# Linear attention and two dense layers: grouped small products, a third fill bank, a reciprocal kept in PSUM, later output transposes

## The chip, the cores and the metric

One NeuronCore of a Trainium2 chip runs the whole kernel. The metric is the device time of one execution in microseconds (us). Five engines work side by side, each with its own queue of instructions: TensorE (PE, with its weight loads shown apart as PEld), VectorE (DVE), ScalarE (ACT), GpSimd (POOL) and SyncE (SP), which here only issues DMAs.

## The reference

Three layers follow one another (B = 4 sequences, H = 8 heads, S = 768 tokens, D = 48; 3072 tokens of 384 numbers).

```python
# 1 gated linear attention
f = 1 / (1 + exp(-f_logit))
for t in range(S):
    state = f[:, :, t, :, None] * state + einsum('bhd,bhe->bhde', k[:, :, t], v[:, :, t])
    y[:, :, t] = einsum('bhd,bhde->bhe', q[:, :, t], state)
# 2 first mix, w_in 384 x 2048, w_out 2048 x 384
h = x @ w_in
P = a[0] + a[1] * h + a[2] * h**2 + a[3] * h**3
Q = 1 + abs(b[0]) * abs(h) + abs(b[1]) * h**2
x = (P / (Q + 1e-06)) @ w_out
# 3 second mix, four experts, w1 384 x 1024, w2 1024 x 384
p = domain_probs / (domain_probs.sum(-1, keepdims=True) + 1e-09)
out = sum(p[:, e:e+1] * (maximum(x @ w1[e], 0) @ w2[e]) for e in range(4))
```

## The kernel before

The tokens go in six chunks, c = 0 to 5; a chunk is 128 time steps of each of the four sequences, so 512 columns. The main loop (L1051 on) counts steps v. Each step from 0 on makes one of the 192 tiles of the second mix (6 chunks x 4 experts x 8 tiles of 128 hidden units): **in2** is the product into the tile, **out2** the product out of it. A number in float32 is split in a high and a low part, so each product is three matmuls; in2 and out2 of a tile are nine matmuls each, 128 x 128 by 128 x 512. `mm_in` issues in2 and in1 at L849, `mm_out` issues out2 and out1 at L859.

Chunk c of the first mix is made while chunk c-1 of the second mix runs: 16 tiles (c, j), each with **in1** into the bank `h1`, a gate on ACT, DVE and POOL, and out1 for four tiles together. The attention of chunk c is woven in as well, in blocks (c, b), one for each sequence, each over six steps (`stage`): scores in the fourth; `k_t` (four transposes of k, L486) and `y_all` (56 small matmuls, L494) in the fifth; `update` (four products of two small matmuls, L528) in the sixth. `fill_run` and `fill_step` put one entry of a list behind each of the nine matmuls of a product: in the fifth stage the list is k_t in the first places (spread over the first three matmuls of out2) and `y_all` behind the sixth; in the sixth stage the four updates stand behind the third, fifth, seventh and ninth matmul of in2.

Chunk 0 has no second mix to run beside. In this **fill** phase `fill_in` (L898, three matmuls of 128 x 512) and `fill_out` (L905) do chunk 0 of the first mix, with the same gate, in float32 without a split.

PSUM has eight banks: `acc` = 0 to 2 for out1 and out2, `hb` = 3 and 4 for in2 (and for fill_in, by turns), `h1` = 5 for in1 (the order listings below call it bank_97; bank_92 is bank 0), 6 and 7 for the attention and for the transposes of the output. In the fill the gate keeps q in banks 5, 6, 7 by turns.

The **gate** of a tile (`gate_in`, `gate_step`) takes two steps. On ACT: a copy h of the bank (L914), q = square (L918), r = scaled abs (L919), y (L920). On DVE: q = Q (L934). On ACT: r = exp(-ln q) (L935, L936). One step later on DVE two refinements of the reciprocal, both reading q and r: L929, and L931 or L938. Then L943 and the split into gh (L945, ACT) and gl (L960, DVE). In the steps with no new gate the order on DVE is L929, L938, L943; the relu's split of in2 (L968 on ACT for gh, L969 on DVE for gl) is queued on the same two engines.

The **output** of chunk c is written in the first steps of chunk c+1. `write_out` (L1026) does three transposes of 128 x 128 (L1028) into bank 6 or 7, a copy to SBUF on ACT (L1035, pool `osp`, two buffers) and a DMA from SP (L1037); it is called for two sequences at a time. Chunk 0 does sequences 0, 1 in step k = 2 ahead of out2 and 2, 3 in the same step behind in2's place; chunks 1 to 4 do 0, 1 in step k = 1, and 2, 3 in step k = 2 ahead of out2. What is transposed is `o`, which POOL sums up (L1004).

Of the kernel before, what the change touches and what calls it, by code (L numbers as in the profile page):

```python
# [8 lines left out]
F32 = mybir.dt.float32  # L9
# [11 lines left out]
NCH = S // C  # L21
NP = NH // 2
# [319 lines left out]
PA, PB, ACT0, ACT1, POOL1, DVE1, REST = range(7)  # L342


def first_mix_steps():


    when, groups = {}, {}
    for c in range(1, NCH):
        p = NE * NJ2 * (c - 1)  # L350
        if c == 1:
            at = [10, 11, 12, 13, 14, 15, 16, 17, 18, 19, 20, 21, 23, 24, 25, 26]
            ends = (16, 20, 24, 29)
        else:
            at = [2, 3, 4, 5] if c == 2 else [-1, 1, 3, 5]
            at += [7, 9, 11, 13, 15, 17, 19, 21, 23, 24, 25, 26]
            ends = (8, 16, 24, 29)
        for j, s in enumerate(at):
            when[p + s] = (c, j)
        for n, s in enumerate(ends):  # L360
            groups[p + s] = (c, n)
    return when, groups
# [37 lines left out]
class Block:  # L400
# [117 lines left out]
    def y_all(self):  # L518
        if self.c:
            self.inter()  # L520
        self.intra()

    def y_parts(self):
        return [self.y_all]

# [32 lines left out]
class Att:  # L558
# [104 lines left out]
    def stage(self, blk, k):  # L663
        rs = range(NP)
        if k == 1:
            return {ACT0: [blk.exp], DVE1: [blk.w], REST: [blk.scans]}
        if k == 2:
            return {ACT0: [blk.inverse], POOL1: [blk.k_hat], DVE1: [blk.newton1], REST: [blk.newton2]}
        if k == 3:
            return {POOL1: [blk.q_hat]}  # L670
        if k == 4:
            return {PA: [blk.all_scores] + [lambda: None] * (8 * (blk.c == 1)), REST: [blk.masked]}
        wait = [lambda: None] * 3
        if k == 5:
            keys = [] if blk.last else [partial(blk.k_t, r) for r in rs]
            copy = [] if blk.last else [blk.k_copy]
            return {PB: keys + wait + blk.y_parts() + wait, REST: copy + [blk.x_hi]}
        if k == 6:
            upd = [] if blk.last else [partial(blk.update, r) for r in rs]
            return {PA: upd, DVE1: [blk.x_lo], REST: [] if blk.last else [blk.finish]}  # L680
        return {}

# [12 lines left out]
def fused(ctx, tc, aps, consts, gm, big, dp, prep, flag_op):  # L695
# [7 lines left out]
    banks = [pp.tile([128, 512], F32, name=f"bank{i}") for i in range(8)]  # L703
    acc, hb, h1 = banks[0:3], banks[3:5], banks[5]
    tok = acc + [h1]

    def pool(name, bufs):
        return ctx.enter_context(tc.tile_pool(name=name, bufs=bufs))
# [3 lines left out]
    g1p, g2p, gp = pool("g1p", QC1), pool("g2p", 3), pool("gp", 2)  # L712
# [8 lines left out]
    raw, temp, w1f = {}, {}, {}  # L721
# [37 lines left out]
    def run_late():  # L759
        for f in late:  # L760
            f()
        late.clear()

    def conv_ops(tau):
        fs = [[], []]
        for i in range(NJ1):
            for k in range(2):
                if tau == CONV1[i] + k * (CONV1[i] >= NB - 6):
                    fs[k].append(partial(conv, i, k))
        return fs  # L770
# [39 lines left out]
    def store_all():  # L810
        for k in stores:
            nc.sync.dma_start(out=scr[uses[k]], in_=tile_of[k].bitcast(F32))
        stores.clear()
# [79 lines left out]
        make_ready(state["used"] + R)  # L893

    def fill_in(j):
        w, ps = w1f[j], hb[j % 2]
        for kk in range(3):
            nc.tensor.matmul(ps, w[:, kk * 128:(kk + 1) * 128], att.x[0][:, kk, :], start=(kk == 0), stop=(kk == 2))  # L898
        gate_queue.append((0, j, ps))
# [6 lines left out]


    gate_queue, gate = [], {}

    def gate_in(u):  # L910
        h = u[2]
        if u[0]:
            h = gp.tile([128, 512], F32, tag="h", name="h")
            nc.scalar.copy(out=h, in_=u[2])  # L914
        q = gp.tile([128, 512], F32, tag="q", name="q", bufs=3) if u[0] else banks[5 + u[1] % 3]
        r = gp.tile([128, 512], F32, tag="r", name="r")
        y = gp.tile([128, 512], F32, tag="y", name="y")
        nc.scalar.activation(out=q, in_=h, func=AF.Square)  # L918
        nc.scalar.activation(out=r, in_=h, func=AF.Abs, scale=sc[:, 4:5])  # L919
        nc.scalar.activation(out=y, in_=h, func=AF.Identity, scale=sc[:, 0:1], bias=sc[:, 1:2])  # L920
        return q, r, y, h
# [104 lines left out]
    def write_out(c, b, bank):  # L1026
        for m in range(3):
            nc.tensor.transpose(bank[:, m * C:(m + 1) * C], o[c][:, m, b * C:(b + 1) * C], ident)  # L1028
        if c == NCH - 1:
            if not last:  # L1030
                last.append(sp.tile([128, NB, DM], F32, tag="s1", name="os"))
            nc.scalar.copy(out=last[0][:, b], in_=bank[:, 0:DM])
            return
        t = osp.tile([128, DM], F32, tag="os", name="os")
        nc.scalar.copy(out=t, in_=bank[:, 0:DM])  # L1035
        r0 = b * S + c * C
        nc.sync.dma_start(out=out[r0:r0 + C, :], in_=t)  # L1037
# [12 lines left out]
    for v in range(-FILL - 6, LAST + 1):  # L1050
        tau = v + FILL  # L1051
        ops = att.begin(v)
        if tau == -4:
            prep()
        if tau + 6 <= NB:
            att.first(tau + 6, conv_ops(tau) if tau + 6 < NB else [[], []], fetch)
        run_late()
        store_all()
        items = steps.get(v, [])
        lead = 1 if items and items[0][0] == "in2" and items[0][1] == v + 1 else 0  # L1060
        fill_run(ops[PA], 9 * lead)
        for item in items[:lead]:
            emit(item)
        if 0 <= v < LAST and v not in act2:
            relu(v)
        for f in ops[ACT0]:
            f()
        for u in gate_queue:
            if u[0] and u[:2] not in gate:
                gate[u[:2]] = gate_in(u)  # L1070
        if 0 <= tau + 1 < NJ1:
            fill_in(tau + 1)
        ready = [u for u in gate_queue if u[:2] in gate]
        new = ready[0] if ready else None
        if new:
            gate_queue.remove(new)
        old, pend_old = pend_old, new
        if new or old:
            gate_step(new, old, ops)
        else:  # L1080
            for f in ops[DVE1] + ops[ACT1] + ops[POOL1]:
                f()
        c, k = v // (NE * NJ2) - 1, v % (NE * NJ2)
        if v in (LAST - 4, LAST - 3):
            for b in range(2):
                write_out(NCH - 1, b + 2 * (v - LAST + 4), banks[6 + b])
        if 0 <= c < NCH - 1 and k == 2:
            for b in range(2):
                write_out(c, b + (2 if c else 0), banks[6 + b])
        fill_run(ops[PB], 9 * any(item[0] == "out2" for item in items), True)  # L1090
        for item in items[lead:]:
            if item[0] == "out2":
                emit(item)
                if run_bounds(v - 1)[1]:
                    evac2(v - 1)
        for item in items[lead:]:
            if item[0] == "in2":
                emit(item)
                if v + 1 < LAST:
                    relu(v + 1)  # L1100
        if 0 <= c < NCH - 1 and k == (1 if c else 2):
            for b in range(2):
                write_out(c, b + (0 if c else 2), banks[6 + b])
        for item in items[lead:]:
            if item[0] == "out1":
                emit(item)
        for item in items[lead:]:
            if item[0] == "in1":
                emit(item)
        for u in gate_queue:  # L1110
            if not u[0] and u[:2] not in gate:
                gate[u[:2]] = gate_in(u)
        if tau == -1:
            spread_probs()
        if 0 <= tau - 2 < NJ1:
            fill_out(tau - 2)
        for f in ops[REST]:
            f()
        if v in groups:
            evac1(*groups[v])  # L1120
        if tau + 6 >= NB:
            for f in sum(conv_ops(tau), []):
                f()
            run_late()
        if 10 <= tau and v < -1:
            make_ready(min(R - 6, 2 * (tau - 9)))
            split_to(min(AHEAD, state["ready"] - 2))
        if tau == NJ1 + 1:
            for m in range(3):
                split_x2(0, m, acc[m], nc.vector)  # L1130
            load_pb(0)
        if v >= -1:
            split_to(state["used"] + AHEAD)
        att.loads(v)
        if v == 170:
            flag_op(banks[6], banks[7])
# [178 lines left out]
```

## Time and profile before

| | |
|---|---|
| median of 3 runs | 1376.14 us (1375.05 to 1377.79) |
| the profiled execution | 1374.64 us |
| its span, first to last instruction | 1372.8 us |
| granted TensorE clock, mean | 0.991 |
| PE busy | 1331.0 us, 97% |
| DVE busy | 870.0 us, 63% |
| ACT busy | 663.0 us, 48% |
| POOL busy | 287.2 us, 21% |
| HBM | 211 GB/s over the span |

The span is what the trace shows; around it lie 1.8 us of the execution's own time. A wait is read from the idle time of an engine ahead of an instruction, with the instruction that ended it. An engine that is busy less than the span can still set the time in the places where it is late.

### The profile page before, as it was taken

The numbers are of one execution on the slowest core, as the hardware profiler recorded it, in microseconds if no ns is written. First come the engines' busy times: TensorE is split into PE (matmuls) and PEld (weight loads), VectorE is DVE, ScalarE is ACT, GpSimd is POOL, SyncE is SP. The second block draws the span as 40 slices with busy tenths as digits, with TensorE's granted clock in tenths as the row PEclk, the third lists the DMA queues.
The fourth block names the chain that finished last, engine by engine and source line by source line (L and its number), as shares of the span: only waits on it lengthen the run. The fifth ranks groups of instructions, "written<-read, shape, count | busy, mean of one in ns | idle before, by whom it ended". The sixth has DMA issues, their size and how long they took to land.

```text
span 1372.8 us, 19580 instructions
## 1 busy us (share of the span) xinstructions
PE 1331.0 (97%) x7158; PEld 1061.8 (77%) x7158; DVE 870.0 (63%) x1367; ACT 663.0 (48%) x1152; POOL 287.2 (21%) x257
## 2 busy tenths in 40 slices
PE   6799999899999999999999999999999999999998
PEld 6444788777787888788888878888888888888887
DVE  8899658677748565757666667576576555552221
ACT  4787448666536445426444435554445453431111
POOL 0233655565420020120110111001111001111010
PEclk9999999999999999999999999999999999999999
DMA  8547877677875666667655758566657666667660
GB/s 312 186 157 269 281 248 255 223 246 249 311 254 178 198 217 188 191 187 244 215 175 194 225 163 266 192 203 195 216 167 252 187 198 193 195 194 239 194 192 31
DMA packets 115704, 291.03 MB, mean 212 GB/s; under 512 B 13104, under 2 KB 28816, under 8 KB 114832
## 3 DMA queue, kind: packets, MB, share of 16 engines
q1 hardware_dynamic: 115024, 289.51, 65.2%
q8 instruction: 59, 0.97, 0.3%
q14 instruction: 45, 0.37, 0.1%
q10 hardware_dynamic: 576, 0.18, 0.1%
HBM read 240.83 MB, written 48.81 MB: 211 GB/s over the span
## 4 chain that ended last, share of the span: by engine, by line


## 5 line engine op out<-in xcount | busy, mean ns | idle before, releaser
L849 PE MATMUL bank<-x,w 128*128 128x512 f32 x2448 | 602.6, 393 | 5.1 <-DVE gl L969 5.1
L849 PEld LDWEIGHTS bank<-x,w 128*128 128x128 f32 x2448 | 455.5, 188 | 99.1 <-DVE gl L969 6.3
L859 PE MATMUL bank<-gh,w 128*128 128x512 f32 x1584 | 502.5, 397 | 5.5 <-DVE t L1003 5.5
L859 PEld LDWEIGHTS bank<-gh,w 128*128 128x128 f32 x1584 | 293.9, 189 | 70.9 <-DVE t L1003 6.8
L859 PE MATMUL bank<-gl,w 128*128 128x512 f32 x792 | 311.4, 393 | 0.0
L969 DVE SCALAR_TENSOR_TENSOR gl<-bank,gh 128x512 fp32r<-128x512 f32 x192 | 131.5, 686 | 152.9 <-ACT gh L968 152.5
L1004 POOL TENSOR_TENSOR o<-o,t 128x512 f32<-128x512 f32 x69 | 89.0, 1320 | 531.9 <-DVE t L1003 531.9
L859 PEld LDWEIGHTS bank<-gl,w 128*128 128x128 f32 x792 | 149.5, 189 | 32.0
L968 ACT ACTIVATE gh<-bank 128x512 fp32r<-128x512 f32 x192 | 113.7, 594 | 124.6 <-PE bank L849 124.6
L934 DVE SCALAR_TENSOR_TENSOR q<-q,sc,r 128x512 f32<-128x512 f32 x80 | 62.1, 776 | 144.6 <-ACT r L919 144.6
L945 ACT CAST gh<-q 128x512 fp32r<-128x512 f32 x80 | 49.2, 615 | 185.2 <-DVE q L943 185.1
L806 POOL TENSOR_TENSOR w<-rawbuf,w 128x384 fp32r<-128x384 f32 x96 | 104.5, 1115 | 89.2 <-ACT w L805 64.7
L914 ACT COPY h<-bank 128x512 f32<-128x512 f32 x80 | 46.9, 586 | 116.3 <-PE bank L849 115.8
L1021 DVE TENSOR_TENSOR s<-s,bank 128x512 f32<-128x512 f32 x45 | 30.9, 687 | 84.7 <-PE bank L859 84.6
L960 DVE TENSOR_TENSOR gl<-q,gh 128x512 fp32r<-128x512 f32 x80 | 55.9, 699 | 33.8 <-ACT gh L945 33.6
L935 ACT ACTIVATE r<-q,sc 128x512 f32<-128x512 f32 x80 | 58.0, 724 | 25.7 <-DVE q L934 19.0
L929 DVE SCALAR_TENSOR_TENSOR q<-q,r 128x512 f32<-128x512 f32 x80 | 69.5, 869 | 0.1
L920 ACT ACTIVATE y<-h,sc 128x512 f32<-128x512 f32 x80 | 64.1, 801 | 0.0
L943 DVE SCALAR_TENSOR_TENSOR q<-y,sc,q 128x512 f32<-128x512 f32 x80 | 62.2, 778 | 1.8
L936 ACT ACTIVATE r<-r 128x512 f32<-128x512 f32 x96 | 60.7, 633 | 3.1
L955 DVE SCALAR_TENSOR_TENSOR y<-y,sc,h 128x512 f32<-128x512 f32 x80 | 60.2, 752 | 2.8
L953 DVE TENSOR_TENSOR y<-y,h 128x512 f32<-128x512 f32 x80 | 57.2, 715 | 0.0
(113 smaller groups left out, 1242.6 us busy)
## 6 DMA issues: line engine op xcount, KB each, us to landing
w<-ws SPq DMA_DIRECT2D x448, 384.0 KB, 3.6
ws<-w SPq DMA_DIRECT2D x96, 384.0 KB, 4.1
raw<-in_w_dram SPq DMA_DIRECT2D x16, 768.0 KB, 6.8
rawbuf<-in_w_dram SPq DMA_DIRECT2D x64, 192.0 KB, 3.6
v<-in_v_dram SPq DMA_DIRECT2D x24, 320.0 KB, 4.5
f<-in_qkf_dram SPq DMA_DIRECT2D x24, 256.0 KB, 3.9
k<-in_qkf_dram SPq DMA_DIRECT2D x24, 256.0 KB, 4.5
q<-in_qkf_dram SPq DMA_DIRECT2D x24, 256.0 KB, 4.6
```

The lines of the kernel that those rows point to most:

```text
L806: nc.gpsimd.tensor_tensor(out=t[:, 1], in0=r, in1=t[:, 0].bitcast(F32), op=ALU.subtract)
L849: nc.tensor.matmul(ps, a[:, o], b[:, kk, :], start=(n == 0), stop=(n == 8))
L859: nc.tensor.matmul(acc[m], a[:, o], b, start=(start and n == 0), stop=(stop and n == last))
L920: nc.scalar.activation(out=y, in_=h, func=AF.Identity, scale=sc[:, 0:1], bias=sc[:, 1:2])
L929: vec.scalar_tensor_tensor(out=q0, in0=q0, scalar=QC, in1=r0, op0=ALU.add, op1=ALU.mult)
L934: vec.scalar_tensor_tensor(out=q, in0=q, scalar=sc[:, 5:6], in1=r, op0=ALU.mult, op1=ALU.add)
L936: nc.scalar.activation(out=r, in_=r, func=AF.Exp, scale=-1.0)
L943: vec.scalar_tensor_tensor(out=q0, in0=y0, scalar=sc[:, 3:4], in1=q0, op0=ALU.subtract, op1=ALU.mult)
L955: vec.scalar_tensor_tensor(out=y, in0=y, scalar=sc[:, 2:3], in1=h, op0=ALU.subtract, op1=ALU.mult)
L968: nc.scalar.activation(out=gh, in_=h, func=AF.Relu)
L969: nc.vector.scalar_tensor_tensor(out=gl, in0=h, scalar=0.0, in1=gh.bitcast(F32), op0=ALU.max, op1=ALU.subtract)
L1004: nc.gpsimd.tensor_tensor(out=o[c][:, m], in0=o[c][:, m], in1=t, op=ALU.add)
```

## The change

Four things change.

1. In the fifth stage k_t (all four) and `y_all` become one entry behind the sixth matmul of out2 (`keys_and_y`); in the sixth stage the four updates become one entry behind the fifth matmul of in2 (`all_updates`).
2. In the fill, `fill_in` goes round three banks (3, 4, 7) and q keeps two (5, 6).
3. A tile whose successor's in1 comes two steps or more later is called sparse (50 of the 80 tiles of chunks 1 to 5). Its r lies in `h1` in place of a tile in SBUF. The successor's in1 overwrites `h1`.
4. `write_out` of chunks 1 to 4 takes chunk 0's pattern: sequences 0, 1 one step later, ahead of out2, and 2, 3 in the same step behind in2's place.

```diff
--- before.py
+++ after.py
@@ -519,6 +519,15 @@
         if self.c:
             self.inter()
         self.intra()
+
+    def keys_and_y(self):
+        for r in range(0 if self.last else NP):
+            self.k_t(r)
+        self.y_all()
+
+    def all_updates(self):
+        for r in range(NP):
+            self.update(r)
 
     def y_parts(self):
         return [self.y_all]
@@ -670,13 +679,12 @@
             return {POOL1: [blk.q_hat]}
         if k == 4:
             return {PA: [blk.all_scores] + [lambda: None] * (8 * (blk.c == 1)), REST: [blk.masked]}
-        wait = [lambda: None] * 3
+        idle = [lambda: None]
         if k == 5:
-            keys = [] if blk.last else [partial(blk.k_t, r) for r in rs]
             copy = [] if blk.last else [blk.k_copy]
-            return {PB: keys + wait + blk.y_parts() + wait, REST: copy + [blk.x_hi]}
+            return {PB: 5 * idle + [blk.keys_and_y] + 3 * idle, REST: copy + [blk.x_hi]}
         if k == 6:
-            upd = [] if blk.last else [partial(blk.update, r) for r in rs]
+            upd = [] if blk.last else 4 * idle + [blk.all_updates] + 4 * idle
             return {PA: upd, DVE1: [blk.x_lo], REST: [] if blk.last else [blk.finish]}
         return {}
 
@@ -893,7 +901,7 @@
         make_ready(state["used"] + R)
 
     def fill_in(j):
-        w, ps = w1f[j], hb[j % 2]
+        w, ps = w1f[j], (banks[3], banks[4], banks[7])[j % 3]
         for kk in range(3):
             nc.tensor.matmul(ps, w[:, kk * 128:(kk + 1) * 128], att.x[0][:, kk, :], start=(kk == 0), stop=(kk == 2))
         gate_queue.append((0, j, ps))
@@ -906,14 +914,16 @@
 
 
     gate_queue, gate = [], {}
+    tiles = sorted(first_mix_steps()[0].items())
+    sparse = {u for (s, u), (t, _) in zip(tiles, tiles[1:]) if t > s + 1}
 
     def gate_in(u):
         h = u[2]
         if u[0]:
             h = gp.tile([128, 512], F32, tag="h", name="h")
             nc.scalar.copy(out=h, in_=u[2])
-        q = gp.tile([128, 512], F32, tag="q", name="q", bufs=3) if u[0] else banks[5 + u[1] % 3]
-        r = gp.tile([128, 512], F32, tag="r", name="r")
+        q = gp.tile([128, 512], F32, tag="q", name="q", bufs=3) if u[0] else banks[5 + u[1] % 2]
+        r = h1 if u[:2] in sparse else gp.tile([128, 512], F32, tag="r", name="r")
         y = gp.tile([128, 512], F32, tag="y", name="y")
         nc.scalar.activation(out=q, in_=h, func=AF.Square)
         nc.scalar.activation(out=r, in_=h, func=AF.Abs, scale=sc[:, 4:5])
@@ -1086,7 +1096,7 @@
                 write_out(NCH - 1, b + 2 * (v - LAST + 4), banks[6 + b])
         if 0 <= c < NCH - 1 and k == 2:
             for b in range(2):
-                write_out(c, b + (2 if c else 0), banks[6 + b])
+                write_out(c, b, banks[6 + b])
         fill_run(ops[PB], 9 * any(item[0] == "out2" for item in items), True)
         for item in items[lead:]:
             if item[0] == "out2":
@@ -1098,9 +1108,9 @@
                 emit(item)
                 if v + 1 < LAST:
                     relu(v + 1)
-        if 0 <= c < NCH - 1 and k == (1 if c else 2):
+        if 0 <= c < NCH - 1 and k == 2:
             for b in range(2):
-                write_out(c, b + (0 if c else 2), banks[6 + b])
+                write_out(c, b + 2, banks[6 + b])
         for item in items[lead:]:
             if item[0] == "out1":
                 emit(item)
```

What this does to the queues, at three places. Line numbers of the changed kernel are up to ten higher.

PE in the fifth stage of block (2, 0). bank_98 and bank_99 are banks 6 and 7; am is the masked scores, s the state. Before:

```order
L859 MATMUL bank_92<-gh,w 128x512
L486 MATMUL bank_98<-ident,k 128x112 x2
L859 MATMUL bank_92<-gh,w 128x512
L486 MATMUL bank_98<-ident,k 128x112
L859 MATMUL bank_92<-gl,w 128x512
L486 MATMUL bank_98<-ident,k 128x112
L859 MATMUL bank_93<-gh,w 128x512 x2
L859 MATMUL bank_93<-gl,w 128x512
L494 MATMUL bank_99<-q,s_1_140 32x128 x12
```

and changed:

```order
L867 MATMUL bank_92<-gh,w 128x512 x2
L867 MATMUL bank_92<-gl,w 128x512
L867 MATMUL bank_93<-gh,w 128x512 x2
L867 MATMUL bank_93<-gl,w 128x512
L486 MATMUL bank_98<-ident,k 128x112 x4
L494 MATMUL bank_99<-q,s_1_140 32x128 x12
```

The four transposes stand five matmuls later than the first of them did, and no big matmul stands between them.

PE at the in1 of tile (1, 12), which follows the sparse tile (1, 11), with the semaphores that a row waits for. Before:

```order
L859 MATMUL bank_94<-gh,w 128x512 x2
L859 MATMUL bank_94<-gl,w 128x512
L849 MATMUL bank_97<-x,w 128x512 [waits Activation_49]
L849 MATMUL bank_97<-x,w 128x512
L849 MATMUL bank_97<-x,w 128x512 [waits Pool_49]
L849 MATMUL bank_97<-x,w 128x512 x6
L849 MATMUL bank_96<-x_1139,w 128x512 [waits DVE_49]
```

and changed:

```order
L867 MATMUL bank_94<-gh,w 128x512 x2
L867 MATMUL bank_94<-gl,w 128x512
L857 MATMUL bank_97<-x,w 128x512 [waits DVE_49]
L857 MATMUL bank_97<-x,w 128x512
L857 MATMUL bank_97<-x,w 128x512 [waits Pool_49]
L857 MATMUL bank_97<-x,w 128x512 x6
L857 MATMUL bank_96<-x_1139,w 128x512 x2
```

Before, the in1 waits for ACT's copy of the bank (L914); changed, it waits for DVE's second refinement of the tile ahead (L948, L938 before), which reads r in the bank.

ACT in the steps k = 1 and 2 of chunk 2, where the output of chunk 1 is written, up to the second relu of the two steps. Before:

```order
L1035 COPY os<-bank_98 128x384 [waits DMAHW6_49,PE_49]
L1035 COPY os<-bank_99 128x384 [waits PE_49]
L968 ACTIVATE gh<-bank_95 128x512
L914 COPY h<-bank_97 128x512 [waits PE_49]
L918 ACTIVATE q<-h 128x512 [waits Activation_49]
L919 ACTIVATE r<-h,sc 128x512
L920 ACTIVATE y<-h,sc 128x512
L935 ACTIVATE r<-q,sc 128x512 [waits DVE_49]
L936 ACTIVATE r<-r 128x512 [waits Activation_49]
L1035 COPY os<-bank_98 128x384 [waits DMAHW7_49,PE_49]
L1035 COPY os<-bank_99 128x384 [waits DMAHW0_49,PE_49]
L968 ACTIVATE gh<-bank_96 128x512
```

and changed:

```order
L930 ACTIVATE y<-h,sc 128x512
L945 ACTIVATE bank_97<-q,sc 128x512 [waits DVE_49]
L946 ACTIVATE bank_97<-bank_97 128x512 [waits Activation_49]
L1045 COPY os<-bank_98 128x384 [waits DMAHW6_49,PE_49]
L1045 COPY os<-bank_99 128x384 [waits PE_49]
L1045 COPY os<-bank_98 128x384 [waits DMAHW2_49,PE_49,Activation_49]
L1045 COPY os<-bank_99 128x384 [waits DMAHW3_49,PE_49,Activation_49]
L978 ACTIVATE gh<-bank_96 128x512
```

Four copies stand in a row ahead of the relu. The pool has two buffers, so the third and fourth copy wait for the landing of the DMAs that the first and second started; before, the DMAs of the first pair were started a whole step ahead of the second pair's copies.

## Rows read from the trace of the kernel before

**Rows 1.** The page, part 1: busy time, share of the span, instructions.

```profile
PE 1331.0 (97%) x7158; PEld 1061.8 (77%) x7158; DVE 870.0 (63%) x1367; ACT 663.0 (48%) x1152; POOL 287.2 (21%) x257
```

**Rows 2.** Waits on PE: tile and line, releaser: us in total, times, longest us.

```profile
PE bank L849 <- DVE gl L969: 5.1, 3, 2.3
...
PE bank L898 <- DVE y L955: 3.9, 2, 3.1
PE bank L486 <- DVE am L481: 2.9, 3, 1.6
PE bank L1028 <- POOL o L1004: 2.2, 3, 0.8
```

**Rows 3.** Timeline of PE, block (2, 0): start us, us, line, [idle before <-releaser].

```profile
336.00 0.40 PE L859 MATMUL bank<-gh,w 128*128 128x512 f32 x1
...
340.40 2.89 PE L849 MATMUL bank<-x,w 128*128 128x512 f32 x12
343.13 0.34 PE L528 MATMUL bank<-v,kt 128*112 128x96 f32 x2
...
343.80 0.34 PE L528 MATMUL bank<-v,kt 128*112 128x96 f32 x2
```

**Rows 4.** Timeline of PE, block (1, 0): k_t and y already together.

```profile
136.64 2.07 PE L849 MATMUL bank<-x,w 128*128 128x512 f32 x8
...
140.69 0.97 PE L849 MATMUL bank<-x,w 128*128 128x512 f32 x3
```

**Rows 5.** Timeline of PE: the longest wait ahead of k_t.

```profile
430.43 0.41 PE L486 MATMUL bank<-ident,k 112*128 112x112 f32 x2 [1.62 <-DVE am L481]
```

**Rows 6.** Timeline of PE early in the fill.

```profile
58.87 2.84 PE L898 MATMUL bank<-x,wf 128*128 128x512 f32 x6 [3.10 <-DVE y L955]
```

**Rows 7.** Busy time in a window of the fill: PE, PEld, DVE, ACT, POOL, PEclk, DMA, GB/s.

```profile
55.50:118.70 63.20, 60.10 (x139) 25.75 (x139) 62.77 (x97) 57.01 (x98) 22.30 (x15) 1.00 0.48 168
```

**Rows 8.** Groups by line on DVE: xcount | busy, mean ns of one | idle before.

```profile
L969 DVE SCALAR_TENSOR_TENSOR gl<-bank,gh 128x512 fp32r<-128x512 f32 x192 | 131.5, 686 | 152.9 <-ACT gh L968 152.5
...
L929 DVE SCALAR_TENSOR_TENSOR q<-q,r 128x512 f32<-128x512 f32 x80 | 69.5, 869 | 0.1
```

**Rows 9.** Timeline of PE and DVE: in1 of (1, 12), refinements of (1, 11).

```profile
311.47 2.20 PE L849 MATMUL bank<-x,w 128*128 128x512 f32 x9
315.74 2.17 PE L849 MATMUL bank<-x,w 128*128 128x512 f32 x7 [2.07 <-DVE gl L969]
...
315.61 1.52 DVE L929 SCALAR_TENSOR_TENSOR q<-q,r 128x512 f32<-128x512 f32 x1
317.16 0.69 DVE L938 SCALAR_TENSOR_TENSOR q<-q,r 128x512 f32<-128x512 f32 x1
```

**Rows 10.** The same behind tiles (2, 5) and (4, 5): refinements and next in1.

```profile
464.12 3.11 PE L849 MATMUL bank<-x,w 128*128 128x512 f32 x13
465.48 0.69 DVE L938 SCALAR_TENSOR_TENSOR q<-q,r 128x512 f32<-128x512 f32 x1
...
897.73 4.01 PE L849 MATMUL bank<-x,w 128*128 128x512 f32 x17
898.98 0.69 DVE L938 SCALAR_TENSOR_TENSOR q<-q,r 128x512 f32<-128x512 f32 x1
```

**Rows 11.** Timeline of ACT, DVE, PE where the output of chunk 1 is written.

```profile
623.72 0.96 ACT L1035 COPY os<-bank 128x384 f32<-128x384 f32 x2
...
624.57 0.61 ACT L968 ACTIVATE gh<-bank 128x512 fp32r<-128x512 f32 x1
...
626.53 0.69 DVE L938 SCALAR_TENSOR_TENSOR q<-q,r 128x512 f32<-128x512 f32 x1
...
628.04 4.24 PE L849 MATMUL bank<-x,w 128*128 128x512 f32 x18
```

**Rows 12.** The DMAs that write the output, all 24 of them.

```profile
DMA to landing us min/median/max: 1.9/3.2/6.0
```

**Rows 13.** Busy time in a window behind 315.74, columns as in rows 7.

```profile
317.00:321.00 4.00, 4.00 (x22) 2.93 (x21) 2.26 (x4) 2.33 (x6) 1.22 (x2) 0.57 0.38 120
```

## Prediction, made before the changed kernel ran

> **What bounds the kernel now.** The page's busy shares come first [rows 1]: PE works 97% of the span and no other engine over two thirds, so the sum of what PE does and waits for is the time, and every term below is a change of PE's work or of a wait on PE. The waits on PE say where it stands still [rows 2]; those left out there are the start's, which the change doesn't touch. A wait has its place in the timeline, where one sees what the releaser did before it. Then the groups by line, for what one instruction costs. The fill is the exception: there DVE is busy 62.77 of 63.20 us [rows 7], and it sets the pace.
>
> The sum is made against the profiled execution, 1374.64 us (span 1372.8), which lies 1.5 below the median of the three runs; the 1.5 is added at the end.
>
> **Part 1, grouping.** Twelve big matmuls in a row last 2.89 us and one 0.40 [rows 3], so from start to start it is (2.89 - 0.40) / 11 = 0.226. In block (2, 0) the out2 of the fifth stage takes 340.40 - 336.00 = 4.40 us [rows 3]; its nine matmuls are 2.04, so spread k_t and y cost 2.36. In block (1, 0) they already stand together, behind eight matmuls (1.81): 140.69 - 136.64 - 1.81 = 2.24 [rows 4]. The matmul that follows there starts while the group drains, so of the 0.12 I take 0.1 as the gain, in 15 blocks 1.5. An update alone between two pairs of matmuls costs 343.80 - 343.13 - 2 x 0.226 = 0.22 [rows 3]; four together show nowhere in the loop. Bounds: no gain, or 0.1 a block as for k_t; I take half, 0.05 x 16 = 0.8. **-2.3**.
>
> k_t five matmuls later gives 5 x 0.226 = 1.1 us more time for the masks on DVE: of the three waits of 2.9 us [rows 2] the longest, 1.62 [rows 5], keeps 0.5, the others go. **-2.4**. The kt copy on ACT starts as much later, and its readers come a step later; no cost.
>
> **Part 2, third bank.** What PE waits for in the fill is 3.9 us, 3.10 of it at 58.87 [rows 2, 6], where a matmul waits for the bank's last reader on DVE. With three banks fill_in runs ahead there. But fill_out needs the gate of its tile, and DVE turns out one gate a step without a pause [rows 7]: PE comes earlier to a wait for the gate. The fill ends when DVE ends: 0. What I charge is a fall of the clock behind that longer wait: between 0 and 1.7 (priced in part 4), half of it, **+0.8**.
>
> Here a rule speaks the other way. The Trainium skill (Perfetto Trace Analysis, Matmuls) says that independent groups of matmuls should rotate through different banks, so that the evacuation of one overlaps the matmuls of the next. By it the third bank would take the 3.9 us of waits away; it is a rival below.
>
> **Part 3, r in the bank.** L929 reads two tiles in SBUF and takes 0.869 us on average; L969, with one operand in PSUM, 0.686 [rows 8]. The worst places are like 315.61, 1.52 us against 0.69 for the next refinement [rows 9]. With r in the bank I take 0.69. DVE has idle time elsewhere, 152.9 us ahead of L969 alone [rows 8], so this counts only where PE waits for DVE.
>
> It makes such places. The next in1 may not start before L938 of the tile ahead is over; before, ACT's copy was enough, microseconds earlier. I compared the end of L938 with the start of the next in1 for all 50 sparse tiles. Those that come out late:
> - (1, 11): L938 ends at 317.85, with the quicker L929 at 317.0; in1 started at 311.47 [rows 9]. So in1 moves to 317.0 and the in2 behind it from 315.74 to 319.1: 3.4 late, the 2.07 that it waited being used up. The longest wait of that line, 2.3 us [rows 2], comes some 50 us behind and can give some back: between 1.1 and 3.4. **+2.2**.
> - (2, 5) and (4, 5): L938 ends at 466.17 and 899.67, the in1s started at 464.12 and 897.73 [rows 10]: 2.0 each, less 0.7 for the quicker refinement. **+2.6**, from 0 to 4.0.
> - Five more, each under 0.4 after that relief, as I read the same view. **+1.2**, from 0 to 2.
>
> **Part 4, output a step later.** Removed: PE's wait of 2.2 us in three places for POOL's sums [rows 2], which by then are done. **-2.2**. The transposes, copies and DMAs stay as many. Moved past: on SP the second pair's DMAs now wait for the third and fourth copy, and the loads of k, q and weights behind them come up to 2 us later; no weight load is among the waits on PE [rows 2], and k and q are used on POOL a step ahead of PE, so 0. On ACT four copies stand in a row, and the third waits for the landing of a DMA that the first started. Behind it on ACT stands the relu, behind that on DVE gl (L979), then both refinements (L939, L948), and PE's next in1 waits for the second one.
>
> Chunk 1's output: the first copies began at 623.72, right behind L936 [rows 11]. Without the earlier pair's copies (about 1) and POOL's wait (0.7) that is about 621.8; the second DMA starts when both copies are done, 622.7 (they take 0.96). Let it land L later. Then the last copy 0.58 with its semaphore, relu 0.64, gl 0.66, two refinements 1.41: L948 ends at 626.0 + L. The in1 at 628.04 [rows 11] would come at 627.3, without the 0.7. It waits L - 1.3. L is 1.9 to 6.0, median 3.2 [rows 12]; the DMAs of these very chunks (1 to 3; chunk 4 has no gate beside it) lie somewhat over the median, and I take 3.6: three waits of 2.3. **+7.0**, from 1.8 to 14.
>
> By the fixed cost of a DMA that the Trainium skill gives (DMA: Bandwidth & Descriptors, Anatomy of one DMA, about 2.0 us) L would be near the low end and the three waits 2.1 us in all. No row here shows a landing under 1.9, and most are longer, so the rows decide.
>
> The sparse tiles two gates behind, (3, 2) and (4, 2), are late by about a microsecond each in the same view, part of which the earlier wait hides. **+1.0**, from 0 to 2.
>
> Clock: behind the wait of 2.07 at 315.74 the granted clock was 0.57 for 4 us [rows 13]: 4 x 0.43 = 1.7 lost. I expect that behind one or two of the three new waits: **+2.5**, from 0 to 5.1.
>
> **Sum.** Losses 0.8 + 2.2 + 2.6 + 1.2 + 7.0 + 1.0 + 2.5 = 17.3; gains 2.3 + 2.4 + 2.2 = 6.9; net +10.4. 1374.64 + 10.4 + 1.5 = **1386.5 us**. With every unknown at its low end the net is about -1, at its high end over +20.
>
> **Rivals.**
> - **DVE's head start** (ends faster). In place of 1.52 us the refinement takes 0.69, and DVE is idle a third of the time; if it also draws ahead through the quicker reads before each of these places, L948 is over when in1 comes. Then only the gains are left: 1374.64 - 6.9 + 1.5 = 1369. For it: all of these places lie beside POOL's work, where the SBUF reads are slow. Against it: at (2, 5) and (4, 5) DVE would need 2.0 us and the quicker read gives 0.7. It decides at 2 us of gain per place. Chance 0.2.
> - **The landing is short** (no change). With L = 1.9 part 4 costs 1.8 and no clock: 1386.5 - 5.2 - 2.5 = 1378.8; if (1, 11) is repaid in full, 1377. Against it the median of 3.2 [rows 12]. 0.15.
> - **The clock falls behind every new wait**, five of 1.3 us and more: five times 1.7 in place of 1.5 times, 1386.5 + 6 = 1392.5. 0.12.
> - **The third bank pays** as that rule has it: 1386.5 - 3.9 - 0.8 = 1382. Against it, DVE without a pause [rows 7]. 0.05.
>
> **Numbers.** The forecast itself has 0.48; 0.2% is 2.75 us, about what a measurement can tell here. Slower by more: forecast, clock and bank, 0.65. Within: the short landing, 0.15. Faster: DVE's head start, 0.2. The range goes from 1369, where the gains stand alone, to 1394, beyond the clock's rival; the forecast's own range is 1381 to 1392.
>
> **What would show it.** In the waits on PE a new row, in1 waiting for DVE's second refinement, at least six places, of 1 us or more and the largest near 5 at tile (1, 12); three of them two steps into a chunk, with ACT's third copy waiting for an output DMA. The row for POOL's o gone; that for k_t down to about 0.5. L939 in the loop near 0.7 us. In the fill, PE's wait moved from fill_in to fill_out, its end unmoved. It is wrong if that new row is under 3 us in all, or if the fill ends over 2 us earlier.

## The result and the profile after

The changed kernel took 1383.5 us in the median of six runs (1381.12 to 1385.64), the kernel before 1375.6 (1371.69 to 1377.79); the ratio is 1.0055, 95% interval 1.0037 to 1.0073. It is 7.9 us slower, where 10.4 were forecast. The profiled executions lie 9.9 apart (1384.49 and 1374.64). Single executions of 1663 us and more are left out of the times and ratios below.

The page's first part, for [rows 1]: PE's busy time is 1.4 us more, DVE's 12 less. The rest of the loss is time in which PE stands still.

```profile
PE 1332.4 (96%) x7158; PEld 1062.3 (77%) x7158; DVE 857.9 (62%) x1367; ACT 661.0 (48%) x1152; POOL 284.0 (21%) x257
```

The waits on PE of the changed kernel, which answer to [rows 2]:

```profile
PE bank L857 <- DVE q L948: 14.0, 7, 5.3
PE bank L494 <- DVE am L481: 11.9, 4, 7.4
...
PE bank L913 <- DVE g L958: 3.6, 2, 2.6
PE bank L857 <- DVE gl L979: 2.9, 3, 1.8
...
PE bank L486 <- DVE am L481: 0.4, 1, 0.4
```

The first row is new: seven in1s wait 14.0 us for the second refinement of the tile ahead. The row for POOL's o is gone, that for k_t fell from 2.9 to 0.4. In the fill the wait of fill_in (L898, 3.9) became one of fill_out for the gate (L913, 3.6).

The timeline at the in1 of (1, 12), for [rows 9]: both refinements take 0.7 us, and the in1 starts when the second is over, after the longest wait of the loop.

```profile
317.37 0.67 DVE L939 SCALAR_TENSOR_TENSOR q<-q,bank 128x512 f32<-128x512 f32 x1
...
318.07 0.69 DVE L948 SCALAR_TENSOR_TENSOR q<-q,bank 128x512 f32<-128x512 f32 x1
...
318.81 6.12 PE L857 MATMUL bank<-x,w 128*128 128x512 f32 x18 [5.31 <-DVE q L948]
```

The timeline where chunk 1's output is written, for [rows 11]. The second DMA starts at 623.26, inside the SP row, and lands at 627.23 (rows of other work are left out):

```profile
622.32 0.86 ACT L1045 COPY os<-bank 128x384 f32<-128x384 f32 x2
...
622.83 0.81 SPq L1047 DMA_DIRECT2D out_dram<-os  x2
...
626.87 0.94 ACT L1045 COPY os<-bank 128x384 f32<-128x384 f32 x2 [3.69 <-DMA out_dram<-os]
...
627.71 0.60 ACT L978 ACTIVATE gh<-bank 128x512 fp32r<-128x512 f32 x1
...
628.34 0.69 DVE L979 SCALAR_TENSOR_TENSOR gl<-bank,gh 128x512 fp32r<-128x512 f32 x1 [5.81 <-ACT gh L978]
...
628.95 0.68 DVE L939 SCALAR_TENSOR_TENSOR q<-q,bank 128x512 f32<-128x512 f32 x1
...
629.66 0.69 DVE L948 SCALAR_TENSOR_TENSOR q<-q,bank 128x512 f32<-128x512 f32 x1
...
630.40 4.37 PE L857 MATMUL bank<-x,w 128*128 128x512 f32 x18 [2.45 <-DVE q L948]
```

That is the chain of part 4, link by link: copies, landing, copies, relu, gl, two refinements, in1. The in1 waits 2.45 us at its end.

To see where the time went I took each big matmul's start in both traces and the difference: how late the changed kernel is at the same place of the program. A wait adds to it, a wait that is gone takes from it.

| place (us in the trace of before) | late by, us | what lies ahead of it |
|---|---|---|
| 45.9, first fill_in | 1.77 | the start: a wait for am of 7.4 in place of 5.2 |
| 136.0, first product of chunk 1 | 2.45 | the fill, +0.7 |
| 307.2 | 1.89 | grouping, about -0.1 a stage |
| 325.7 | 4.52 | tile (1, 11): +5.1 at the in2 behind it, 2.4 back by here |
| 377.4 | 2.85 | later waits grown shorter |
| 436.7 | 1.39 | the wait ahead of k_t |
| 611.4 | 0.71 | k_t -0.9; (2, 5) +0.35, (2, 8) +0.35 |
| 645.7 | 4.34 | chunk 1's output and tiles behind it |
| 863.2 | 6.94 | k_t -0.9, (3, 5) +0.5, (3, 8) +0.35, chunk 2's output |
| 1067.4 | 9.02 | (4, 5) +1.3, (4, 8) +0.35, chunk 3's output |
| end | 9.78 | (5, 8) +0.35, the last steps |

The first 1.8 us belong to no part of the change: the first fill_in of the kernels here lies between 45.0 and 47.7 us. From the first product of chunk 1 to the end the loss is 7.3 us, near the 7.9 of the medians. Below, "in the loop" means this stretch, against the trace of before.

### The profile page after: what moved, and what is told of

It is laid out like the page before. It is cut to its first block, busy times and chain, and to the rows that moved or that the text cites. A ratio compares the mean times of both kernels' runs of the same rounds, so it can differ in the third digit from the quotient of the medians.

```text
span 1382.6 us, 19566 instructions
## 1 busy us (share of the span) xinstructions
PE 1332.4 (96%) x7158; PEld 1062.3 (77%) x7158; DVE 857.9 (62%) x1367; ACT 661.0 (48%) x1152; POOL 284.0 (21%) x257
## 4 chain that ended last, share of the span: by engine, by line
## 5 line engine op out<-in xcount | busy, mean ns | idle before, releaser
L867 PE MATMUL bank<-gh,w 128*128 128x512 f32 x1584 | 494.5, 393 | 5.1 <-DVE t L1013 5.1
L944 DVE SCALAR_TENSOR_TENSOR q<-q,sc,bank 128x512 f32<-128x512 f32 x50 | 37.3, 747 | 109.4 <-ACT bank L929 109.4
L1013 DVE TENSOR_TENSOR t<-bank,pb 128x512 f32<-128x512 f32 x69 | 44.8, 685 | 15.1 <-PE bank L867 14.9
L928 ACT ACTIVATE q<-h 128x512 f32<-128x512 f32 x80 | 50.6, 632 | 2.5
L451 POOL TENSOR_TENSOR k<-k,g 112x512 f32<-112x512 f32 x20 | 26.6, 1331 | 117.8 <-DMA k<-in_qkf_dram 67.1
```

What stands on the lines that cost most here:

```text
L867: nc.tensor.matmul(acc[m], a[:, o], b, start=(start and n == 0), stop=(stop and n == last))
```

## The experiments

Each run is timed against the kernel before on its own chip; a ratio is to that. The diffs name what differs from the changed kernel or from the kernel before.

**r back in SBUF.**

```diff
-        r = h1 if u[:2] in sparse else gp.tile([128, 512], F32, tag="r", name="r")
+        r = gp.tile([128, 512], F32, tag="r", name="r")
```

> The changed kernel with r always in SBUF (grouping, third bank and later output stay). Theory A (the loss is in1's wait for DVE's second refinement, which only r in the bank of in1 makes): the row of 14.0 us of waits on L948 goes whole, some of it comes back as older waits for gl (about 2), so about 1383.5 - 12 = 1371.5 us, ratio to before 0.997. Theory B (the four copies in a row make the relu late, and PE then waits for gh or gl of out2, wherever r lies): 4 to 6 us of waits remain in the steps behind a chunk's start, about 1377.

1373.67 us, ratio 0.9978 (0.9964 to 0.9992). The 14.0 us are gone, and in the loop the kernel stands 0.3 us ahead of before, 7.6 ahead of the changed one. The time lies between the two theories, because PE now waits for other things:

```profile
PE bank L857 <- DVE gl L979: 8.5, 7, 2.5
...
PE bank L1038 <- ACT os L1045: 2.9, 3, 1.0
```

Most of the first row are the kernel before's waits for gl come back; 1.6 us of it is one wait in chunk 5, behind the output of chunk 4. The timeline at chunk 1's output shows the second row's cause. A refinement with r in SBUF took 1.66 us beside POOL, so the gate, and behind it ACT's copies, were late, and the second transposes, which go into the same two banks, waited for them:

```profile
613.03 1.66 DVE L948 SCALAR_TENSOR_TENSOR q<-q,r 128x512 f32<-128x512 f32 x1
...
620.50 0.84 ACT L1045 COPY os<-bank 128x384 f32<-128x384 f32 x2
...
621.01 0.93 PE L1038 MATMUL bank<-ident,o 128*128 128x128 f32 x6 [0.98 <-ACT os L1045]
```

**No landing to wait for.** The second pair's copies take their buffers from the pool of t, those of chunk 0's output too.

```diff
-        t = osp.tile([128, DM], F32, tag="os", name="os")
+        t = (osp if b < 2 else tp).tile([128, DM], F32, tag="os" if b < 2 else "t", name="os")
```

> The changed kernel, but the second pair of output copies takes its buffers from another pool, so no copy waits for the landing of the first pair's DMAs. Theory A (the landing is the long link of the chain that delays in1 behind a chunk's start): the waits of 2.45, 2.06 and the third one of the kind (about 630, 850 and 1062 us) fall under 0.4 each; the waits two gates on (1.5 at 642 and 1066) stay or grow by some tenths, as DVE is not put off before; in all 3 to 5 us less than the changed kernel, 1379 to 1380. Theory C (r in the bank alone makes these waits): no change, 1383.

1371.52 us, ratio 0.9969 (0.9954 to 0.9983): 2.2 us ahead of before in the loop, 9.6 ahead of the changed kernel, twice what I expected. The three waits at tile 1 (2.45, 2.06 and 1.50 us) are gone; of the next gate's, which I thought would stay, the one of 1.5 fell to 0.9, and one of 0.9 came in the next chunk. About 2 us are the clock: in the changed kernel the stretch with the wait of 2.06 became 4.0 us late. Another 0.6 us lie at chunk 0's output. At the same place as above the third copy no longer waits for the DMA, and in1 for nothing:

```profile
618.04 0.86 ACT L1045 COPY os<-bank 128x384 f32<-128x384 f32 x2
...
619.32 0.86 ACT L1045 COPY os<-bank 128x384 f32<-128x384 f32 x2 [0.41 <-PE bank L1038]
...
622.03 0.69 DVE L948 SCALAR_TENSOR_TENSOR q<-q,bank 128x512 f32<-128x512 f32 x1
...
623.52 4.24 PE L857 MATMUL bank<-x,w 128*128 128x512 f32 x18
```

**r in the bank alone**, on the kernel before:

```diff
-        r = gp.tile([128, 512], F32, tag="r", name="r")
+        r = h1 if u[:2] in sparse else gp.tile([128, 512], F32, tag="r", name="r")
```

> The kernel before with r in the bank for the 50 sparse tiles and nothing else of the change. Theory A: waits on L948 at tile (1, 11) of about 5, at (3, 2), (4, 2) of over 1, at (2, 5), (3, 5), (4, 5) and four small ones; 9 to 10 us of waits, of which 3 to 4 replace older waits: 5 to 7 us slower than before, 1381 to 1382.5. Theory D (the quicker refinements beside POOL help as much): within 2 us of before.

1382.81 us, ratio 1.0058 (1.0036 to 1.0079), 6.5 us late in the loop. The waits on L940 (L938 before) are 8.6 us, 5.3 of it at (1, 12), in five places where I had expected about ten. Theory A holds:

```profile
PE bank L849 <- DVE q L940: 8.6, 5, 5.3
```

**The third bank alone**, on the kernel before:

```diff
-        w, ps = w1f[j], hb[j % 2]
+        w, ps = w1f[j], (banks[3], banks[4], banks[7])[j % 3]
-... else banks[5 + u[1] % 3]
+... else banks[5 + u[1] % 2]
```

> The kernel before with three banks in the fill and nothing else. Theory A (DVE sets the fill's pace; PE's wait moves to the end, where the clock falls): the first scores of chunk 1 start 0 to 0.8 us later against the start of the fill, 1376. Theory E (rotating banks lets the evacuation overlap the next product): they start about 3.9 us earlier, 1372.

1374.88 us, ratio 0.999 (0.9978 to 1.0003): no difference. From the first fill_in to the first product of chunk 1 it is 0.2 us shorter than before. fill_in ran 3.6 us ahead from 62 us on, and all of it was lost at the last gates, for which fill_out waited:

```profile
PE bank L905 <- DVE g L948: 3.2, 2, 2.3
```

So it is in the changed kernel, whose timeline shows the longer of these waits, and its window behind it (columns as in [rows 7]) the clock's lower level:

```profile
130.61 4.54 PE L913 MATMUL bank<-g,wf 128*128 128x512 f32 x6 [2.65 <-DVE g L958]
```

```profile
132.00:134.00 2.00, 2.00 (x3) 0.76 (x3) 1.85 (x3) 0.63 (x1) 1.27 (x1) 0.50 1.05 421
```

**Later output alone**, on the kernel before:

```diff
-                write_out(c, b + (2 if c else 0), banks[6 + b])
+                write_out(c, b, banks[6 + b])
...
-        if 0 <= c < NCH - 1 and k == (1 if c else 2):
+        if 0 <= c < NCH - 1 and k == 2:
             for b in range(2):
-                write_out(c, b + (0 if c else 2), banks[6 + b])
+                write_out(c, b + 2, banks[6 + b])
```

> The kernel before with the later output of chunks 1 to 4 and nothing else; r in SBUF. Theory A (as the run without r in the bank showed: the first pair's copies on ACT come late because a refinement beside POOL takes 1.6 us, and chunk 5 waits for a relu behind a landing): saves POOL's 2.2 us, pays three waits of about 0.9 of the second transposes for ACT's copies and 1 to 2 us early in chunk 5: 0 to 2.5 us slower than before, 1376 to 1378.5. Theory G (only POOL's wait counts): 2.2 us faster, 1373.5.

1379.51 us, ratio 1.0021 (1.0010 to 1.0033). In the loop 3.9 us late, more than either theory. POOL's 2.2 us are gone, the three waits for ACT's copies are there (2.9 us), and chunk 5 paid 0.7. Behind chunk 1's output alone the kernel lost 2.8 us: the fourth copy waited for a landing until 631.69, the relu and gl behind it came late, and an in2 waited for a gl.

```profile
631.69 0.48 ACT L1035 COPY os<-bank 128x384 f32<-128x384 f32 x1 [2.44 <-DMA out_dram<-os]
...
638.08 0.67 DVE L969 SCALAR_TENSOR_TENSOR gl<-bank,gh 128x512 fp32r<-128x512 f32 x1
...
638.80 2.35 PE L849 MATMUL bank<-x,w 128*128 128x512 f32 x9 [0.82 <-DVE gl L969]
```

So the landing can reach PE without r in the bank too, by way of the relu and gl.

**Grouping alone**, on the kernel before, with the two new functions:

```diff
-            return {PB: keys + wait + blk.y_parts() + wait, REST: copy + [blk.x_hi]}
+            return {PB: 5 * idle + [blk.keys_and_y] + 3 * idle, REST: copy + [blk.x_hi]}
...
-            upd = [] if blk.last else [partial(blk.update, r) for r in rs]
+            upd = [] if blk.last else 4 * idle + [blk.all_updates] + 4 * idle
```

> Grouping alone. By the prediction's terms: 2.3 us less PE work and 2.4 us less waiting ahead of k_t, 4.7 us faster than before, about 1371; each block's fifth stage 0.1 us and each sixth stage 0.05 us shorter in the trace. Theory H (a group between big matmuls costs as much as its parts, only the waits go): 2.4 to 3 us faster, 1373.

1371.77 us, ratio 0.9974 (0.9959 to 0.9989), 4.8 us ahead in the loop, against the prediction's -4.7. The wait ahead of k_t is down to 0.5; another kind of wait, for t, rose from 5.5 to 6.7:

```profile
PE bank L867 <- DVE t L1013: 6.7, 3, 4.3
...
PE bank L486 <- DVE am L481: 0.5, 1, 0.5
```

**Grouping and later output from two pools**: the run before, with the diff of later output and this:

```diff
-        t = osp.tile([128, DM], F32, tag="os", name="os")
+        t = (osp if b < 2 else tp).tile([128, DM], F32, tag="os" if b < 2 else "t", name="os")
```

> Grouping and later output with buffers from two pools; r in SBUF, two banks in the fill. Theory A: no wait for a landing is left, three waits of 0.9 for ACT's copies stay, POOL's 2.2 go, grouping gives 4 to 5: 4 to 5 us faster than before, 1371. If r in the bank is of no use at all (theory C), it is as fast as or faster than the next run.

1371.69 us, ratio 0.9968 (0.9957 to 0.9979), 5.3 us ahead in the loop; L1038 waits 2.9 us for ACT's os, as expected.

**r in the bank where it can't be waited for**, two pools:

```diff
-    sparse = {u for (s, u), (t, _) in zip(tiles, tiles[1:]) if t > s + 1}
+    sparse = {u for (s, u), (t, _) in zip(tiles, tiles[1:]) if t > s + 1 and u[1] not in (2, 5, 8) and u != (1, 11)}
```

> The changed kernel with two pools for the output, and r in the bank only for the sparse tiles whose successor's in1 did not wait: without tiles 2, 5 and 8 of a chunk and without (1, 11). Theory A: the rows of waits on L948 are gone (8.3 us with two pools and all sparse tiles), 2 to 3 of it come back as older waits at chunk 1's end; the refinement beside POOL at tile 0 of a chunk stays 0.69, so the second transposes don't wait for ACT: 5 to 7 us less than with all sparse tiles, 1365 to 1367, ratio 0.992 to 0.994. Theory C (r in the bank is of no use): 1371, as the run without it.

1365.04 us, ratio 0.9924 (0.9910 to 0.9938): faster than both kernels, and where theory A had it; 10.5 us ahead in the loop. No in1 waits for a refinement, no transpose for ACT. Its waits on PE, without the start's:

```profile
PE bank L867 <- DVE t L1013: 5.8, 3, 4.3
PE bank L857 <- DVE gl L979: 5.0, 4, 2.1
...
PE bank L913 <- DVE g L958: 3.2, 2, 2.3
PE bank L470 <- POOL q L466: 1.1, 1, 1.1
```

**The same with one pool of two buffers:**

```diff
-        t = (osp if b < 2 else tp).tile([128, DM], F32, tag="os" if b < 2 else "t", name="os")
+        t = osp.tile([128, DM], F32, tag="os", name="os")
```

> The fastest kernel so far (r in the bank for selected tiles, output from two pools) with one pool of two buffers again. Theory A (the landing is what makes r in the bank dear at a chunk's start): three waits on L948 of 2 to 2.5 us at tile 1 of chunks 3 to 5 come back, with the clock's fall behind one of them, and a relu behind a landing in chunk 5: 7 to 9 us slower than with two pools, 1372 to 1374. Theory C2 (the waits at the excluded tiles were all that cost): within 2 us of it, 1365 to 1367.

1376.12 us, ratio 0.9994 (0.9983 to 1.0005): 11 us slower than with two pools, 13 in the loop. The waits came back at the three places, 6.4 us in all. Behind two of them the clock fell, and in the trace the stretch with the wait of 2.38 became 4.3 us late, that with 2.51 4.4 us, the third with 1.47 only 1.8. That is 10.5 us; 1.8 more were lost at chunk 0's output, which loses its second pool too, and 0.8 in chunk 5:

```profile
626.00:628.00 2.00, 2.00 (x6) 1.58 (x5) 2.00 (x6) 0.40 (x2) 0.25 (x1) 0.50 0.69 255
...
844.00:846.00 2.00, 2.00 (x6) 1.54 (x6) 1.92 (x4) 1.11 (x2) 0.00 (x0) 0.50 1.03 348
```

**r in the bank for tile 0 only**, with grouping, later output, two pools and two banks in the fill:

```diff
-    sparse = {u for (s, u), (t, _) in zip(tiles, tiles[1:]) if t > s + 1}
+    sparse = {u for (s, u), (t, _) in zip(tiles, tiles[1:]) if t > s + 1 and u[1] == 0}
```

> Grouping, later output, two pools, two banks in the fill, and r in the bank only for tile 0 of chunks 2 to 5. Theory A (the refinement beside POOL at tile 0, 1.6 us with r in SBUF, delays ACT's first output copies, for which the second transposes wait): the waits of L1038 on ACT's os, 2.9 us in three places, go, all else is as without r in the bank: about 3 us faster than that kernel, measured from the first product of chunk 1 on. Rival: the waits stay near 0.9 each, since ACT's own gate work sets when the copies come.

1366.18 us, ratio 0.9922 (0.9905 to 0.9940), 9.6 us ahead in the loop, 4.2 more than with r in SBUF throughout (the run of grouping and later output from two pools), where I had expected about 3. The waits of L1038 are gone: at chunk 1's output the refinement took 0.69 us where it had taken 1.67, and ACT's copies came 2.1 us behind the transposes where it had been 3.4.

```profile
610.44 0.69 DVE L948 SCALAR_TENSOR_TENSOR q<-q,bank 128x512 f32<-128x512 f32 x1
...
615.40 0.82 PE L1038 MATMUL bank<-ident,o 128*128 128x128 f32 x6
...
617.53 0.84 ACT L1045 COPY os<-bank 128x384 f32<-128x384 f32 x2
```

and with r in SBUF throughout:

```profile
612.70 1.67 DVE L948 SCALAR_TENSOR_TENSOR q<-q,r 128x512 f32<-128x512 f32 x1
...
616.80 0.82 PE L1038 MATMUL bank<-ident,o 128*128 128x128 f32 x6
...
620.18 0.84 ACT L1045 COPY os<-bank 128x384 f32<-128x384 f32 x2
```

**Tile (1, 11) left out** of the changed kernel's sparse tiles:

```diff
-    sparse = {u for (s, u), (t, _) in zip(tiles, tiles[1:]) if t > s + 1}
+    sparse = {u for (s, u), (t, _) in zip(tiles, tiles[1:]) if t > s + 1 and u != (1, 11)}
```

> The changed kernel with r of tile (1, 11) in SBUF, else unchanged. The wait of 5.3 us at tile (1, 12) goes and 2.1 for gl comes back at the in2 behind it; with what later waits take up, between 360 and 590 us of the span the kernel is 1.0 to 2.2 us less late than the changed one.

1380.28 us, ratio 1.0032 (1.0020 to 1.0045). The wait went and 2.08 for gl came back. Relative to the stretch ahead of the tile it stands 1.7 us better than the changed kernel at 370 us, but from 425 to 600 us only 0.7 to 0.8: less than expected. It is 3.2 us faster in the median; of the 4.2 us between the two profiled executions 3.4 lie ahead of the loop, where the kernels don't differ.

## Why the prediction was right, and where its terms were off

The forecast was 1386.5 and slower; the measured 1383.5 lies in the range, with the loss at the places named. The forecast's net was 10.4, the measured 7.9. Of the signs, the new row came out at 14.0 us, with the largest wait at (1, 12), but five of its waits are of 1 us or more, not six.

Two of its sums don't come out as written. The low ends of the losses add up to 2.9 us (1.1 and 1.8), so with gains of 6.9 the lowest net is -4, not -1. And 623.72 less 1 and 0.7 is 622.0, not 621.8, which would make each wait for a landing L - 1.1. The main sum holds.

| part | forecast, us | alone, in the loop | remark |
|---|---|---|---|
| grouping | -4.7 | -4.8 | |
| third bank | +0.8 | -0.2 in the fill | +0.7 in the changed kernel's profile |
| r in the bank | +6.0, and 1.0 of part 4 | +6.5 | |
| later output | -2.2, +7.0, +2.5 | +3.9 | with r in the bank dearer |
| together | +10.4 | +7.3 | |

Part 1. The sum came as worked out, its terms both a little larger. In the changed kernel three blocks of chunk 1 (148 to 197 us) gain 0.18 each, for the 0.15 forecast, and the three places with a wait ahead of k_t gain 1.25, 0.92 and 0.91 (0.09 of each is k_t's grouping), for 2.4 in all; a fourth place, ahead of y, gains 0.49. In the run of grouping alone, waits for t that grew by 1.2 took some of it back.

Part 2. DVE sets the fill's pace, as the forecast said. The rule of the Trainium skill (Perfetto Trace Analysis, Matmuls) names what happened first: with the third bank the wait for the bank's reader went (the row of 3.9 us on L898). The 3.9 us did not come out of the time, as each product's result had still to pass DVE. So the trace doesn't bear the rule out here, and the rival built on it fell.

Part 3. The mechanism and the places were right; single sizes were off both ways. (4, 5) cost 1.3 as forecast, (2, 5) 0.35 in place of 1.3: before, a DVE instruction of that tile ran beside POOL for 1.75 us, and in the changed kernel it fell outside POOL's time and took 0.69, which I had counted for the refinement only. The small places cost 0.35 to 0.5 each, for 0.24. The step that failed is the 2.2 for (1, 11). At the in2 behind it the kernel came 5.1 us later for the 3.4 worked out, as in1 ran at the clock's lower level. Of that only 0.7 was left, by the run without this tile. Given back were not only some of the wait at 360 us (2.32 to 1.84), which I had set against it, but the whole of one at 326 us (0.59) and the clock: in the kernel before it fell twice here with PE at work, at 317 us [rows 13] and behind the wait at 360 us, in the changed kernel once, partly inside the long wait. The windows behind 360 us, before and changed:

```profile
362.00:364.00 2.00, 2.00 (x6) 1.51 (x6) 1.95 (x5) 1.06 (x3) 0.00 (x0) 0.50 0.95 342
```

```profile
363.00:365.00 2.00, 1.12 (x5) 0.95 (x6) 1.97 (x4) 1.18 (x2) 1.28 (x1) 1.00 1.00 327
```

So the 0.7 is no fixed price. With two pools the clock stayed up behind that wait in both kernels, and leaving the tile out gave 2.4 us (the run with selected tiles against that with all of them, at 370 us).

Part 4. The three waits were 2.45, 2.06 and 1.50, with the second DMAs landing 3.97, 3.61 and 3.02 us after their start: L - 1.5, where L - 1.3 was forecast, and L a little under the 3.6 I took. 6.0 for 7.0. The Trainium skill (DMA: Bandwidth & Descriptors, Anatomy of one DMA) gives about 2.0 us as the fixed cost of a DMA issued from GpSimd. The output's DMAs are issued from SP; the least that showed is 1.9, and at these places the landings were longer in all three. The clock fell behind one of the three, at 850 us; 2.5 was for one or two. Of (3, 2) and (4, 2) the first made a wait of 1.50, the second none.

What the forecast missed is in "DVE's head start", given 0.2. The quicker read is worth something, but not at the tiles for which I counted it. It is worth 4.2 us at tile 0 of a chunk, ahead of the output's copies. In the changed kernel this gain is inside: its transposes don't wait for ACT. The forecast has no term for that wait, though the second transposes go into the banks that the first copies read. That the term of -2.2 held is luck: later output alone put 2.9 us of waits for ACT in the place of POOL's 2.2, and only the quicker read at tile 0 keeps them away. Grouping, r in the bank and later output add up to 5.6 alone and to 7.3 together: the gain at tile 0 makes the sum smaller, the landing's cost behind r in the bank makes it larger. The other rivals: the landing was not short, and the clock didn't fall behind every wait.

That the landing and the bank work together is shown by pairs with and without two pools. In the loop two pools are worth 9.6 us with all sparse tiles, 13 with the selected ones, and 5.0 with r in SBUF throughout (the run with r back in SBUF against that of grouping and later output from two pools, which has two banks in the fill). Where the output of chunks 1 to 3 is written, between 611 and 1067 us, it is 8.1, 10.5 and 1.3. So the landing costs something wherever r lies, and several times as much with r in the bank. What decides whether the clock falls behind a wait was not tried, and stays open.

## What to carry to other kernels

Before a scratch value goes into the bank of a product, compare the end of its last reader with the start of the next product there, tile by tile; the reader that matters is the last, not the copy that used to free the bank. Two steps moved together on one queue need as many buffers as they have transfers, or the later one puts a DMA's round trip ahead of everything queued behind it. A bundle is worth taking apart: the same four parts, with r in the bank only where no product waits for it and the second pair's buffers from another pool, are 0.76% faster than before in place of 0.55% slower.

## What the runs showed that was not expected

The same wait of 3.10 us early in the fill with two banks was followed by full clock in three of six profiles, and by the lower level in three. The window from 61 to 63 us of the kernel before and of the run with later output alone:

```profile
61.00:63.00 2.00, 2.00 (x6) 0.92 (x5) 2.00 (x4) 2.00 (x4) 1.25 (x1) 1.00 0.88 366
```

```profile
61.00:63.00 2.00, 2.00 (x4) 0.97 (x3) 2.00 (x4) 2.00 (x5) 1.51 (x1) 0.50 0.96 399
```

Where it fell for longest (twice) the fill took 2.4 us more. The third bank takes this wait away and has a shorter fall at the fill's end in six of seven profiles; their fills lie between 0.7 us shorter and 0.7 longer than that of the kernel before. In the loop, too, in the changed kernel, the wait of 2.45 us was not followed by a fall and that of 2.06 was:

```profile
632.00:634.00 2.00, 2.00 (x11) 1.65 (x10) 2.00 (x6) 0.40 (x2) 0.12 (x1) 1.00 0.85 280
```

```profile
852.00:854.00 2.00, 2.00 (x6) 1.58 (x5) 2.00 (x6) 0.45 (x1) 0.00 (x0) 0.50 0.81 312
```

A read of two SBUF tiles on DVE beside POOL took from 0.68 to 1.67 us, where the same instruction with r in PSUM took at most 0.69, beside POOL too. In the changed kernel the groups show it, first with r in the bank, then in SBUF:

```profile
L939 DVE SCALAR_TENSOR_TENSOR q<-q,bank 128x512 f32<-128x512 f32 x50 | 33.9, 677 | 0.1
...
L939 DVE SCALAR_TENSOR_TENSOR q<-q,r 128x512 f32<-128x512 f32 x30 | 27.3, 908 | 0.0
```
